# The widths of the last chunk's blocks and the step of the later chunks' exponentials, in an attention-and-two-MLPs kernel

## The chip, the cores and the metric

The kernel runs on one core of one Trainium2 chip. The metric is the device time of one execution in microseconds (us), as the median of several runs; the core's engines are TensorE (matrix products), VectorE, ScalarE, GpSimd and SyncE (it only issues DMAs). In the profile they are PE (matmuls) and PEld (the weight loads that go before them), DVE, ACT, POOL and SP.

## What is computed

12,480 tokens of width 128 pass through three stages. First an attention over 32 learned vectors ("inducing"), then an MLP with the activation h·cos(h), then an MLP with the activation h·sigmoid(h). Both MLPs go from 128 to 2048 and back to 128.

```python
def mab(q, kv):
    s = scale * (q @ kv.transpose(0, 2, 1))
    s = s - s.max(-1, keepdims=True)
    a = np.exp(s)
    a /= a.sum(-1, keepdims=True) + 1e-09
    return a @ kv
h = mab(I, x)                       # 32 x 128
x = mab(x, h)                       # 12480 x 128
h1 = x @ w_in1;  x = (h1 * np.cos(h1)) @ w_out1
h2 = x @ w_in2;  x = (h2 / (1 + np.exp(-h2))) @ w_out2
```

## The kernel before

A prologue of some 45 us loads x, transposes it and builds the 32 vectors h (the first `mab`). The rest, lines 724 to 1075, is a pipeline that this case is about.

**Tiling.** The 12,480 tokens are 98 tiles (97 whole ones and half a tile), and a tile is cut in four groups of 32 tokens. Tiles are gathered in seven chunks: 8 tiles, five times 16, and 10. A chunk is the unit of the second `mab`'s softmax. Its scores are 128 partitions (four groups of 32) by the chunk's columns, 512 for a chunk of 16 tiles.

A block is the unit of the MLPs: up to 512 token columns, given as pieces (group, first tile, tiles). The chunks of 16 tiles make four blocks of 512 columns each, one per group. The last chunk has 10 tiles with one group a little short, 1216 columns in all, and makes three blocks, numbers 22 to 24 of 25. Before the change these have 480, 448 and 288 columns (lines 263 to 267).

**Steps.** The 2048 hidden units are taken 256 at a time, so a block has eight units. The loop `for s in range(NU + L2 + D2 + 1)` does one step per unit; there are 200 units. In a full step TensorE runs 20 matmuls of the block's width, each with 128x128 fresh weights:

- `mlp1_in(s)`: 2 matmuls (line 763). ScalarE then makes the sine (798); VectorE multiplies (802), rounds to `hi` (809) and subtracts to `lo` (835).
- `mlp2_in(s - 11)`: 6 matmuls (line 898). ScalarE then makes the Silu (913) and `hi` (921), and GpSimd the `lo` (922).
- `mlp2_out(s - 13)`: 6 matmuls (`down`, line 845).
- `mlp1_out(s - 1)`: 6 matmuls (`down`, line 845).

All instructions stand in program order on their engine, by hand. The two accumulators of the down products have one PSUM buffer each, so the first matmul of a block's `mlp1_out` or `mlp2_out` waits until the block before has been read out of it.

**What comes at fixed steps of eight.** After `mlp2_out` of a block's last unit, at steps with s mod 8 = 4, `store` transposes the second accumulator on VectorE (945) and issues the output DMAs on SyncE (955, 961): four for each piece of the block, and one more where a piece holds the half tile. After `mlp1_out` of a block's last unit, at s mod 8 = 0, `y_split` copies the first accumulator: `yhi` on ScalarE (879), `ylo` on VectorE (880); from step 11 on it stands behind the step's `lo` (835) on VectorE. `fill` lets SyncE copy the softmax into a block's stacked operand, four DMAs a piece (298).

**The softmax of chunks 2 to 6** is spread over twelve steps that begin 24 steps before the chunk's first unit. For chunk 2 (whose first unit is step 48; 32 steps later for each of the next four) the table `later` puts "take" at step 24, "centre" at 26, "exp" at 28, "norm" at 30, "turn" at 34, "split" at 35. "exp" is one ScalarE instruction (243), issued right after the step's sine. "norm" is three VectorE instructions (247 to 249), issued at the end of its step, and a GpSimd multiply (250).

`held_back` moves `mlp2_in` of nearby steps to a later place among the matmuls: in the step after "exp" it goes to place 2, behind `mlp2_out` and `mlp1_out`; in the second step after it, and in the step after "take", to place 1, behind `mlp2_out`.

Of the kernel before, what the change touches and what calls it, by code (L numbers as in the profile page):

```python
# [22 lines left out]
def tile_induced_attention_then_two_mlps(  # L23
# [45 lines left out]
    FIRST, LAST, MT = 8, 10, 4  # L69
# [190 lines left out]
    blocks, first_of = [], []  # L260
    for k, (t0, nt) in enumerate(chunks):
        first_of.append(len(blocks))
        if k == NK - 1:
            half = nt // 2
            blocks += [(k, [(0, t0, nt), (3, t0, half)])]
            blocks += [(k, [(1, t0, nt), (3, t0 + half, nt - half)])]
            blocks += [(k, [(2, t0, nt)])]
        elif k > 0:
            blocks += [(k, [(g, t0, nt)]) for g in range(G)]
        else:  # L270
            for t in range(t0, t0 + nt, MT):
                m = min(MT, t0 + nt - t)
                blocks.append((k, [(g, t, m) for g in range(G)]))
# [30 lines left out]
    with ExitStack() as pro:  # L304
# [266 lines left out]
        for i in range(1, end):  # L571

            k = i - 2
# [164 lines left out]


    second = {3: "take", 5: "centre", 12: "exp", 12.25: "norm", 13: "turn", 14: "split"}  # L740
    later = {0: "take", 2: "centre", 4: "exp", 6: "norm", 10: "turn", 11: "split"}

    def d1(u):
        return 2 if u < WHOLE1 else 1
# [365 lines left out]
```

## Time and profile before

| | us |
|---|---|
| median of 3 runs (lowest, highest) | 958.15 (957.73, 958.24) |
| the profiled execution's own time | 957.71 |
| its span, first to last instruction | 955.5 |
| PE busy | 941.5 (99%) |
| DVE busy | 778.2 (81%) |
| ACT busy | 691.9 (72%) |
| POOL busy | 516.1 (54%) |

The granted TensorE clock has a mean of 0.999 of full speed. The engines run beside each other, so their busy times don't add up to the span. PE's matmuls overlap: one is listed with a duration longer than the distance to the next one, so what a matmul costs is read from the distance of starts and not from the durations.

### The profile page before, as it was taken

The numbers are of one execution on the slowest core, as the hardware profiler recorded it, in microseconds if no ns is written. First come the engines' busy times: TensorE is split into PE (matmuls) and PEld (weight loads), VectorE is DVE, ScalarE is ACT, GpSimd is POOL, SyncE is SP. The second block draws the span as 40 slices with busy tenths as digits, with TensorE's granted clock in tenths as the row PEclk, the third lists the DMA queues.
The fourth block names the chain that finished last, engine by engine and source line by source line (L and its number), as shares of the span: only waits on it lengthen the run. The fifth ranks groups of instructions, "written<-read, shape, count | busy, mean of one in ns | idle before, by whom it ended". The sixth has DMA issues, their size and how long they took to land.

```text
span 955.5 us, 11951 instructions
## 1 busy us (share of the span) xinstructions
PE 941.5 (99%) x4480; PEld 757.7 (79%) x4481; DVE 778.2 (81%) x784; ACT 691.9 (72%) x725; POOL 516.1 (54%) x274
## 2 busy tenths in 40 slices
PE   8899999999999999999999999999999999999997
PEld 5456778888878888878888887888887888888896
DVE  4889888988887988887988887988888888878751
ACT  5688668777768777767777777777767777777774
POOL 3346545655545655554655554665554655555565
PEclk9999999999999999999999999999999999999999
DMA  9341000010010010010010010010010100100001
GB/s 346 127 139 45 4 20 11 9 25 18 5 22 12 12 23 12 12 22 12 12 23 12 12 22 12 12 23 9 14 22 1 23 17 6 21 14 4 12 11 21
DMA packets 65484, 28.19 MB, mean 30 GB/s; under 512 B 54440, under 2 KB 60040, under 8 KB 65416
## 3 DMA queue, kind: packets, MB, share of 16 engines
q1 hardware_dynamic: 64760, 27.24, 10.9%
q8 instruction: 37, 0.61, 0.3%
q14 instruction: 31, 0.25, 0.1%
q10 hardware_dynamic: 656, 0.09, 0.1%
HBM read 14.79 MB, written 6.39 MB: 22 GB/s over the span
## 4 chain that ended last, share of the span: by engine, by line
PE 96%; DMA 2%; DVE 1%; issue 0%; ACT 0%; SPq 0%; POOL 0%; ACTq 0%; POOLq 0%; DVEq 0%
PE acc L845 53%; PE h L898 28%; PE h L763 9%; PE acc L855 4%; DMA x_sb<-in_x_dram 2%; PE s L213 1%; PE pt L394 0%; PE hp L541 0%; PE s L421 0%; DVE et L509 0%; SPq L330 0%; DVE c L802 0%; DVE mx L434 0%; PE misc L457 0%; POOL lo L927 0%
## 5 line engine op out<-in xcount | busy, mean ns | idle before, releaser
L922 POOL TENSOR_TENSOR lo<-s,hi 128x1024 fp32r<-128x1024 f32 (+3 forms) x189 | 445.6, 2358 | 372.7 <-ACT hi L921 351.9
L845 PE MATMUL acc<-hi,wo 128*128 128x512 f32 (+3 forms) x1520 | 401.7, 386 | 0.0
L845 PEld LDWEIGHTS acc<-hi,wo 128*128 128x128 f32 x1520 | 282.6, 188 | 59.8 <-issue 3.9
L798 ACT ACTIVATE c<-h,half_pi 128x1024 f32<-128x1024 f32 (+3 forms) x200 | 219.2, 1096 | 141.4 <-PE h L763 141.4
L802 DVE TENSOR_TENSOR h<-h,c 128x1024 f32<-128x1024 f32 (+3 forms) x188 | 226.1, 1203 | 115.3 <-ACT c L798 115.0
L913 ACT ACTIVATE s<-h 128x1024 f32<-128x1024 f32 (+3 forms) x200 | 201.1, 1006 | 73.7 <-PE h L898 69.9
L898 PE MATMUL h<-yhi,wi 128*128 128x512 f32 (+3 forms) x800 | 242.5, 385 | 0.0
L845 PE MATMUL acc<-lo,wo 128*128 128x512 f32 (+3 forms) x760 | 230.2, 384 | 0.1
L809 DVE CAST hi<-h 128x1024 fp32r<-128x1024 f32 (+3 forms) x188 | 224.8, 1196 | 6.5
L835 DVE TENSOR_TENSOR lo<-h,hi 128x1024 fp32r<-128x1024 f32 (+3 forms) x188 | 223.9, 1191 | 5.7
L921 ACT CAST hi<-s 128x1024 fp32r<-128x1024 f32 (+3 forms) x189 | 195.9, 1036 | 6.0
L898 PEld LDWEIGHTS h<-yhi,wi 128*128 128x128 f32 x800 | 148.9, 188 | 28.7 <-issue 0.5
L845 PEld LDWEIGHTS acc<-lo,wo 128*128 128x128 f32 x760 | 141.8, 188 | 27.9 <-POOL lo L927 0.4
L898 PE MATMUL h<-ylo,wi 128*128 128x512 f32 (+3 forms) x400 | 153.6, 384 | 0.0
L763 PE MATMUL h<-stk,hw 128*128 128x512 f32 (+3 forms) x400 | 125.8, 396 | 1.4 <-ACT stk L706 0.7
L763 PEld LDWEIGHTS h<-stk,hw 128*128 128x128 f32 x400 | 74.1, 188 | 24.9 <-issue 6.7
L898 PEld LDWEIGHTS h<-ylo,wi 128*128 128x128 f32 x400 | 75.1, 188 | 14.5
L945 DVE STREAM_TRANSPOSE o<-acc 128x512 f32<-128x512 f32 (+3 forms) x25 | 17.3, 693 | 9.4 <-PE acc L845 9.4
L879 ACT CAST yhi<-acc 128x512 fp32r<-128x512 f32 (+3 forms) x25 | 14.4, 577 | 14.0 <-PE acc L845 14.0
L855 PE MATMUL acc<-c,wf 128*128 128x512 f32 x48 | 22.5, 592 | 0.0
L880 DVE TENSOR_TENSOR ylo<-acc,yhi 128x512 fp32r<-128x512 f32 (+3 forms) x25 | 16.7, 668 | 5.4 <-ACT yhi L879 5.3
L802 DVE TENSOR_TENSOR c<-h,c 128x1024 f32<-128x1024 f32 x12 | 14.6, 1215 | 2.4 <-ACT c L798 1.9
(133 smaller groups left out, 318.7 us busy)
## 6 DMA issues: line engine op xcount, KB each, us to landing
out_dram<-o SPq DMA_DIRECT2D x80, 64.0 KB, 1.9
x_sb<-in_x_dram SPq DMA_DIRECT2D x8, 512.0 KB, 9.6
raw<-in_moe_w_in_dram SPq DMA_DIRECT2D x8, 512.0 KB, 7.3
raw<-in_moe_w_out_dram SPq DMA_DIRECT2D x8, 512.0 KB, 4.2
stk<-ahi SPq DMA_DIRECT2D x40, 64.0 KB, 2.0
stk<-at SPq DMA_DIRECT2D x40, 64.0 KB, 2.0
x_sb<-in_x_dram SPq DMA_DIRECT2D x3, 256.0 KB, 3.9
x_sb<-in_x_dram SPq DMA_DIRECT2D x2, 320.0 KB
```

Of the source, the lines that this page charges most:

```text
L763: nc.tensor.matmul(ps[:, a, 0:n], lhsT=hw[f // 4][:, f % 4 * P : (f % 4 + 1) * P], rhs=stacks[b][:, 0:n], start=True, stop=True,)
L798: nc.scalar.activation(cs, h, AF.Sin, bias=half_pi, scale=1.0)
L802: nc.vector.tensor_tensor(cs if whole else h, h, cs, ALU.mult)
L809: nc.vector.tensor_copy(hi[:, :, 0:n], h)
L835: nc.vector.tensor_tensor(lo[:, :, 0:n], h, hi[:, :, 0:n].bitcast(F32), ALU.subtract)
L845: nc.tensor.matmul(acc[:, 0:n], lhsT=wt[:, 2 * j + a, :], rhs=gt[:, a, 0:n], start=(j == 0 and p == 0 and a == 0), stop=(j == NJ - 1 and p ...
L855: nc.tensor.matmul(acc[:, 0:n], lhsT=w[:, 2 * j + a, :], rhs=c[:, a, 0:n], start=(j == 0 and a == 0), stop=(j == NJ - 1 and a == 1),)
L898: nc.tensor.matmul(ps[:, a, 0:n], lhsT=wt[:, fs], rhs=yt[:, 0:n], start=(p == 0), stop=(p == 2),)
L913: nc.scalar.activation(sv, hid2.pop(u)[:, :, 0:n], AF.Silu)
L921: nc.scalar.copy(hv, sv)
L922: nc.gpsimd.tensor_tensor(lv, sv, hv.bitcast(F32), ALU.subtract)
L945: nc.vector.transpose(o.rearrange("p t d -> p (t d)")[:, 0:n], acc2.pop(b)[:, 0:n])
```

## The change

The last chunk's three blocks get 512, 512 and 192 columns. The second block now has three pieces: all of group 1, the last four tiles of group 3 and the first three of group 2; the third block has the other seven tiles of group 2. Block 23 so gets twelve operand DMAs in place of eight and thirteen output DMAs in place of nine. And "exp" and "norm" of chunks 2 to 6 come a step later (29 and 31 for chunk 2); `held_back` is computed from "exp", so its places move with it, to steps 30 and 31.

```diff
         if k == NK - 1:
-            half = nt // 2
-            blocks += [(k, [(0, t0, nt), (3, t0, half)])]
-            blocks += [(k, [(1, t0, nt), (3, t0 + half, nt - half)])]
-            blocks += [(k, [(2, t0, nt)])]
+            cut = nt - MT
+            blocks += [(k, [(0, t0, nt), (3, t0, cut)])]
+            blocks += [(k, [(1, t0, nt), (3, t0 + cut, MT), (2, t0, MT - 1)])]
+            blocks += [(k, [(2, t0 + MT - 1, nt - MT + 1)])]
...
-    later = {0: "take", 2: "centre", 4: "exp", 6: "norm", 10: "turn", 11: "split"}
+    later = {0: "take", 2: "centre", 5: "exp", 7: "norm", 10: "turn", 11: "split"}
```

## Rows read from the trace of the kernel before

**Rows 1.** The page, part 1: busy us, share and instructions of each engine.

```profile
PE 941.5 (99%) x4480; PEld 757.7 (79%) x4481; DVE 778.2 (81%) x784; ACT 691.9 (72%) x725; POOL 516.1 (54%) x274
```

**Rows 2.** The page, part 4: the chain that ended last, by engine.

```profile
PE 96%; DMA 2%; DVE 1%; issue 0%; ACT 0%; SPq 0%; POOL 0%; ACTq 0%; POOLq 0%; DVEq 0%
```

**Rows 3.** Timeline of PE, steps 28 to 30: start us, us, engine, line, operation.

```profile
149.34 0.62 PE L763 MATMUL h<-stk,hw 128*128 128x512 f32 x2
...
153.88 0.61 PE L763 MATMUL h<-stk,hw 128*128 128x512 f32 x2
154.41 1.17 PE L845 MATMUL acc<-hi,wo 128*128 128x512 f32 x4
...
158.61 0.61 PE L763 MATMUL h<-stk,hw 128*128 128x512 f32 x2
```

**Rows 4.** Timeline of DVE, steps 28 to 33.

```profile
153.56 0.70 DVE L945 STREAM_TRANSPOSE o<-acc 128x512 f32<-128x512 f32 x1
...
165.69 0.68 DVE L247 TENSOR_REDUCE sm<-s 128x16 f32<-128x512 f32 x1
...
166.94 1.21 DVE L802 TENSOR_TENSOR h<-h,c 128x1024 f32<-128x1024 f32 x1
...
170.58 1.22 DVE L802 TENSOR_TENSOR h<-h,c 128x1024 f32<-128x1024 f32 x1
...
174.24 0.68 DVE L880 TENSOR_TENSOR ylo<-acc,yhi 128x512 fp32r<-128x512 f32 x1
```

**Rows 5.** Timeline of PE, step 33: its first matmul and its `mlp1_out`.

```profile
172.21 0.61 PE L763 MATMUL h<-stk,hw 128*128 128x512 f32 x2
...
175.38 1.07 PE L845 MATMUL acc<-hi,wo 128*128 128x512 f32 x4
```

**Rows 6.** Timeline of PE, step 192: twelve matmuls of 480 columns, six of 448.

```profile
896.18 0.60 PE L898 MATMUL h<-yhi,wi 128*128 128x480 f32 x2
...
898.79 0.98 PE L845 MATMUL acc<-hi,wo 128*128 128x448 f32 x4
...
900.01 0.30 PE L763 MATMUL h<-stk,hw 128*128 128x288 f32 x1
```

**Rows 7.** Timeline of PE, steps 205 and 207, block 24 alone.

```profile
937.85 0.29 PE L898 MATMUL h<-ylo,wi 128*128 128x288 f32 x1
938.19 0.77 PE L845 MATMUL acc<-hi,wo 128*128 128x288 f32 x4
...
940.63 0.43 PE L898 MATMUL h<-yhi,wi 128*128 128x288 f32 x2
...
942.21 0.29 PE L898 MATMUL h<-yhi,wi 128*128 128x288 f32 x1
```

**Rows 8.** Timeline of PEld and PE, prologue: matmuls of 128 columns with fresh weights.

```profile
43.51 0.52 PEld L699 LDWEIGHTS st<-lo,pick 128*128 128x128 f32 x4
...
43.55 0.62 PE L699 MATMUL st<-lo,pick 128*128 128x128 f32 x4
```

**Rows 9.** Timeline of all engines, the last matmul and what follows it.

```profile
947.66 0.97 POOL L927 TENSOR_TENSOR lo<-s,hi 128x288 fp32r<-128x288 f32 x1 [0.46 <-POOL lo L927]
948.68 0.19 PEld L845 LDWEIGHTS acc<-lo,wo 128*128 128x128 f32 x1 [0.36 <-POOL lo L927]
948.69 0.40 PE L845 MATMUL acc<-lo,wo 128*128 128x288 f32 x1
949.12 0.48 DVE L945 STREAM_TRANSPOSE o<-acc 128x288 f32<-128x288 f32 x1 [1.16 <-PE acc L845]
```

**Rows 10.** Timeline of PE: the last matmul of the last `mlp2_in`.

```profile
946.03 0.30 PE L898 MATMUL h<-ylo,wi 128*128 128x288 f32 x1
```

**Rows 11.** Timeline of DVE: block 23's store, step 204.

```profile
937.39 0.65 DVE L945 STREAM_TRANSPOSE o<-acc 128x448 f32<-128x448 f32 x1 [8.00 <-PE acc L845]
```

**Rows 12.** Timeline of SyncE's queue (SPq): block 23's output DMAs.

```profile
938.07 2.56 SPq L955 DMA_DIRECT2D out_dram<-o  x4
...
941.29 1.90 SPq L955 DMA_DIRECT2D out_dram<-o  x4
```

## The prediction

> **What bounds the kernel now.** I read the page's part 1 first: PE is busy in 99% of the span, no other engine in more than 81% [rows 1]. Then the chain that ended last: 96% of it is PE [rows 2]. So outside the prologue the time is TensorE's, in two kinds: matmuls, each worth the distance from its start to the next start, and the few waits in between. I looked for these by the starts of line 763's first matmul in each step, since a full step has 20 matmuls of 512 columns. Step 28 lasts 153.88 - 149.34 = 4.54 us, or 0.227 a matmul, and nearly all full steps are like it. Step 29 lasts 158.61 - 153.88 = 4.73 [rows 3]. Such a step follows each of the five "exp" steps of chunks 2 to 6 (0.17 to 0.20 us too long each), and besides the steps of the scores, which have more matmuls, no other step of the middle is long.
>
> **The exponentials: what goes.** In step 29 `mlp2_in` is held back, so `mlp2_out` of a new block stands right behind the two matmuls of `mlp1_in`. It would be due at 153.88 + 2 x 0.227 = 154.33. It starts at 154.41 and its first matmuls are slow [rows 3], because it needs the second accumulator, and the transpose of step 28's store runs to 153.56 + 0.70 = 154.26 on VectorE [rows 4]. From the transpose's end to where PE is back on its beat, 154.33 + 0.20 = 154.53, is 0.27. With "exp" at step 29 the held-back steps are 30 and 31, and in step 29 six matmuls (1.36 us) stand between again. The wait goes: 5 x 0.19 = -0.95 us. Nothing is late behind it at steps 30 and 31, as their Silu, `hi` and `lo` come in the same order, one step later.
>
> **The exponentials: what comes.** "norm" moves too, from step 30 to 31, and its VectorE part stands at the end of its step. In before it begins at 165.69, and the next step's multiply at 166.94, so it holds VectorE for 1.25 us [rows 4]. VectorE is already late then, since step 29's sine came late, behind "exp" and a Silu. It works without a gap from there: multiply of step 31 at 166.94, of step 32 at 170.58 (3.64 a step against 4.53, so it wins back 0.9 us a step), `ylo` of step 32 from 174.24 to 174.92 [rows 4]. `ylo` frees the first accumulator, and `mlp1_out` of the next block is due at 175.38, which is 3.17 into step 33 [rows 5]. Here the wait is hidden, by 0.46 us less the 0.27 above.
>
> After the change one step to catch up is missing between "norm" and `ylo`. Count from the start E of the step with "exp" (149.34 in before). "norm" starts 165.69 - 158.61 = 7.08 into its step [rows 3, 4], now the third from E: E + 9.07 + 7.08 = E + 16.15. The next step's multiply comes 1.25 later, at E + 17.40; and from that multiply to the end of `ylo` it is 174.92 - 170.58 = 4.34, so E + 21.74. `mlp1_out` is due at four steps and 3.17: E + 18.13 + 3.17 = E + 21.30. It gets back on its beat at 21.74 + 0.27 = E + 22.01, 0.7 us late. What is queued behind it on PE is the next step's `mlp1_in`, so the whole pipeline is late by it. At 0.69 a chunk: 5 x 0.69 = +3.45 us. Bounds: 0 (VectorE catches up in a way I don't see) and 5 x 1.0 (the wait in full with 0.3 more of lateness).
>
> **The widths.** Each block has 8 units of 20 matmuls, 160. At 480 columns a matmul costs (898.79 - 896.18) / 12 = 0.2175, at 448 (900.01 - 898.79) / 6 = 0.2033 [rows 6], at 288 (942.21 - 940.63) / 12 = 0.1317 [rows 7], at 512 0.227 [rows 3]. Block 22 gains 160 x 0.0095 = +1.52 and block 23 160 x 0.0237 = +3.79, together +5.3 us. All of it is on the path, and the other engines have run full steps of 512 columns all along.
>
> Block 24 at 192 columns is not in the trace. By the line through 288 and 448 it would be 0.089; that is the lower end. But every matmul here has a fresh 128x128 weight load. In the prologue, where such matmuls have only 128 columns, the loads follow each other at (0.52 - 0.19) / 3 = 0.110 us and the matmuls no faster [rows 8, 9]. And at the very end, where a load and its matmul start together (948.68 and 948.69), the matmul lasts 0.40 and not 0.30 [rows 9, 10]: it waits some 0.10 for its weights. So a load takes about 0.11, 288 columns hide it and 192 don't. I take 0.110: 160 x (0.1317 - 0.110) = -3.47. The upper end: the 128 columns could be slow in themselves, at 0.110 / 128 a column, and 192 would take 0.165, dearer than 288. I hold to the load since the last matmul shows it without a narrow one. Net +1.84; ends -1.6 and +10.6.
>
> The Trainium skill ("TensorE: Matmul & The Clock Gate", section LDWEIGHTS) has a load take its columns over 1.2 GHz, an estimate of 0.107 for 128; the rows' 0.110 agree, and by it the net would be +1.4. The same page (section Back-to-back issue gap) gives 0.081 as the sustained spacing at 128 columns; by that the load would not bind at 192, which is the second rival below. The trace's 0.110 speaks against it.
>
> **The end.** From the last matmul of the last `mlp2_in` to the last matmul of all it is 948.69 - 946.03 = 2.66 us [rows 9, 10], by Silu, `hi` and GpSimd's `lo` (0.97), then matmul and transpose (0.48). If only `lo` and transpose shrink with the columns by a third, that is 0.48 less; if all does, 1.1. I take 0.7, of which 18 x 0.022 = 0.39 is already in the matmuls: -0.3. The handover of the second accumulator from block 23 to 24 is exposed now: due at 937.85 + 0.13, `mlp2_out` starts at 938.19, 0.15 after the transpose's end [rows 7, 11]. With the transpose at 0.70 and six covering matmuls at 0.110 in place of 0.132 it is 0.05 + 0.13 worse: +0.2 (0 to 0.3).
>
> **Cost nothing.** Block 23's four more operand DMAs go out behind its eight, on SyncE, which has five steps (over 20 us) for them. Its four more output DMAs cost 4 x 0.48 = 1.9 us of SyncE's queue: they now end at 943.2, some 6 us before the last transpose, which needs their buffer [rows 9, 12]. With block 24 shorter by some 2 us a part of that cover goes, not all; without it each further us would be on the end.
>
> **Sum** against the profiled execution's 957.71 (span 955.5, 2.21 around it): -0.95 + 3.45 + 1.84 - 0.3 + 0.2 = +4.24, so 961.95. The median of the runs stood 0.44 above the profiled one; I put half on top: 962.1.
>
> **Rivals.**
> (a) No new wait at `ylo`: the 0.19 go and nothing comes. 961.95 - 3.45 = 958.5. For it: in before the same handover had 0.19 us to spare [rows 4, 5]. Against it: VectorE's rows have no gap from 166.94 on, so lateness can't go away.
> (b) The weight load doesn't bind at 192 columns (0.089): 160 x 0.021 = 3.4 less, 958.5, not slower than before. It decides from 0.098 a matmul on: below that the time is within 0.2% of before. For it: 288 columns show no sign of a load. Against it: the 0.110 of [rows 8].
> (c) (a) and (b) together: 955.1, faster.
> (d) Narrow matmuls stream at half rate (0.165): 160 x 0.055 = +8.8, 970.8. For it: [rows 8] alone would allow it. Against it: the last matmul [rows 9].
>
> **How the numbers follow.** Forecast 0.64 (960.3 to 963.5), (a) 0.13, (b) 0.12, (c) 0.04, (d) 0.07. The likeliest gives 962.1. The range takes in (a) and (b) and leaves out (c) and (d): 958.0 to 964.5. Under 0.2% (1.9 us) can't be told from no change: slower means over 960.1, which is nearly all of the forecast (0.62) and (d): 0.69; (a) and (b) are no change: 0.25; faster 0.06.
>
> **What would show it.** Right: steps 29, 61, 93, 125, 157 at 4.53; steps 33, 65, 97, 129, 161 at about 5.2, with PE's wait put down to `ylo`; matmuls of block 24 spaced by 0.110; blocks 22 and 23 at 0.227. Wrong: steps 33 and their like at 4.53 (then (a)); a spacing of 0.09 (b) or 0.165 (d) in the last steps; a wait of the last transpose for DMAs.

## The result, and the profile after

The changed kernel takes 963.63 us (median of 4 runs, 962.73 to 964.08) against 957.94 for the kernel before in the same session: a ratio of 1.0057, 95% interval 1.0045 to 1.0070, so 4.3 to 6.7 us slower. The forecast was 962.1 us, slower. The profiled execution after took 962.73 us, with a span of 960.4 against 955.5.

Where the 4.9 us of span lie, by the starts of line 763's matmuls (steps 0 to 24 differ by 0.04):

| stretch | before | after | difference |
|---|---|---|---|
| start to step 0 | 44.90 | 44.64 | -0.26 |
| step 24 to 176 (the moved exponentials) | 695.79 | 697.84 | +2.05 |
| step 176 to the last matmul's start (the new widths) | 122.91 | 125.28 | +2.37 |
| last matmul's start to the end of the span | 6.81 | 7.61 | +0.80 |

The page's part 1 and part 4 after, the lines that answer to [rows 1, 2]:

```profile
PE 944.5 (98%) x4481; PEld 754.3 (79%) x4481; DVE 777.1 (81%) x784; ACT 691.4 (72%) x725; POOL 516.9 (54%) x274
...
PE 89%; DVE 6%; DMA 1%; ACT 1%; issue 1%; SPq 0%; ACTq 0%; DVEq 0%
```

PE's matmuls are the same in number but for one record, yet VectorE now has 6% of the chain, where PE alone had 96% before. A chain that leaves the bounding engine says that there is a wait in it, and the list of PE's waits names it (engine, line, who was waited for: us in total, times, longest):

```profile
PE acc L845 <- DVE ylo L880: 1.4, 5, 0.3
PE acc L845 <- DVE o L945: 0.3, 1, 0.3
```

There are five waits for `ylo`, one for each of chunks 2 to 6, and one for the transpose at the handover from block 23 to 24. Before, this list was empty from 70 us on, though step 29 lost 0.19 there: the list counts only idle time behind the end that the profile models for the matmul before, and in [rows 3] the late matmul starts at 154.41, ahead of that end, 153.88 + 0.61 = 154.49. Step 29 and step 33 on PE's timeline after, to hold against [rows 3, 5]:

```profile
153.58 0.62 PE L763 MATMUL h<-stk,hw 128*128 128x512 f32 x2
...
158.12 0.39 PE L763 MATMUL h<-stk,hw 128*128 128x512 f32 x1
...
171.72 0.62 PE L763 MATMUL h<-stk,hw 128*128 128x512 f32 x2
...
174.44 0.61 PE L845 MATMUL acc<-lo,wo 128*128 128x512 f32 x2
175.35 1.19 PE L845 MATMUL acc<-hi,wo 128*128 128x512 f32 x4 [0.30 <-DVE ylo L880]
176.39 0.63 PE L845 MATMUL acc<-lo,wo 128*128 128x512 f32 x2
176.85 0.39 PE L763 MATMUL h<-stk,hw 128*128 128x512 f32 x1
```

Step 29 is down to 4.54 us, step 33 is up from 4.53 to 176.85 - 171.72 = 5.13 (5.07 to 5.14 in the five). The 0.30 that the row names is only what exceeds the end of the matmul before, as the profile models it; the whole loss, 0.60, is read from the distance of the steps. VectorE's timeline shows why, against [rows 4]; GpSimd's instruction beside it is in the last line:

```profile
168.59 1.23 DVE L835 TENSOR_TENSOR lo<-h,hi 128x1024 fp32r<-128x1024 f32 x1
169.74 0.68 DVE L247 TENSOR_REDUCE sm<-s 128x16 f32<-128x512 f32 x1
170.44 0.32 DVE L248 TENSOR_SCALAR sm<-sm 128x16 f32<-128x16 f32 x1
170.80 0.25 DVE L249 RECIPROCAL sm<-sm 128x16 f32<-128x16 f32 x1
170.97 1.21 DVE L802 TENSOR_TENSOR h<-h,c 128x1024 f32<-128x1024 f32 x1
...
174.62 0.68 DVE L880 TENSOR_TENSOR ylo<-acc,yhi 128x512 fp32r<-128x512 f32 x1
...
168.32 2.42 POOL L922 TENSOR_TENSOR lo<-s,hi 128x1024 fp32r<-128x1024 f32 x1 [0.76 <-POOL lo L922]
```

"norm" at 169.74 is followed directly by the step whose end is `ylo`. `ylo` ends at 175.30, 21.72 after the start of the step with "exp" (153.58); PE's matmul, due at 171.72 + 3.17 = 174.89, starts at 175.35.

Block 24 after: step 200, where twelve wide matmuls stand between narrow ones, and steps 206 to 208, twelve matmuls of 192 columns each ([rows 6, 7] before):

```profile
929.20 0.59 PE L845 MATMUL acc<-hi,wo 128*128 128x192 f32 x4
...
929.85 0.66 PE L898 MATMUL h<-yhi,wi 128*128 128x512 f32 x2
930.34 0.39 PE L898 MATMUL h<-ylo,wi 128*128 128x512 f32 x1
...
932.65 0.59 PE L845 MATMUL acc<-hi,wo 128*128 128x192 f32 x4
...
944.77 0.39 PE L898 MATMUL h<-yhi,wi 128*128 128x192 f32 x2
...
946.12 0.39 PE L898 MATMUL h<-yhi,wi 128*128 128x192 f32 x2
...
948.79 0.39 PE L898 MATMUL h<-yhi,wi 128*128 128x192 f32 x2
```

Step 206 gives (946.12 - 944.77) / 12 = 0.1125 a matmul, the two steps behind it (948.79 - 946.12) / 24 = 0.111. The twelve wide ones between 929.85 and 932.65 take 2.80 us where 12 x 0.227 are 2.72: the first ones behind a narrow group are slow, the first two 930.34 - 929.85 = 0.49 and not 0.45.

### The profile page after: what moved, and what is told of

The parts are those of the page before. It is cut to its first block, busy times and chain, and to the rows that moved or that the text cites. A ratio compares the mean times of both kernels' runs of the same rounds, so it can differ in the third digit from the quotient of the medians.

```text
span 960.4 us, 11960 instructions
## 1 busy us (share of the span) xinstructions
PE 944.5 (98%) x4481; PEld 754.3 (79%) x4481; DVE 777.1 (81%) x784; ACT 691.4 (72%) x725; POOL 516.9 (54%) x274
## 4 chain that ended last, share of the span: by engine, by line
PE 89%; DVE 6%; DMA 1%; ACT 1%; issue 1%; SPq 0%; ACTq 0%; DVEq 0%
PE acc L845 49%; PE h L898 26%; PE h L763 9%; PE acc L855 4%; DMA x_sb<-in_x_dram 1%; DVE hi L809 1%; DVE lo L835 1%; DVE h L802 1%; ACT c L798 1%; PE s L213 1%; ACT s L913 1%; PE hp L541 0%; PE pt L394 0%; DVE sm L247 0%; DVE ylo L880 0%
## 5 line engine op out<-in xcount | busy, mean ns | idle before, releaser
L922 POOL TENSOR_TENSOR lo<-s,hi 128x1024 fp32r<-128x1024 f32 (+1 forms) x189 | 447.3, 2367 | 376.0 <-ACT hi L921 348.8
L845 PE MATMUL acc<-hi,wo 128*128 128x512 f32 (+1 forms) x1520 | 402.6, 387 | 1.7 <-DVE ylo L880 1.4
L798 ACT ACTIVATE c<-h,half_pi 128x1024 f32<-128x1024 f32 (+1 forms) x200 | 219.3, 1097 | 144.8 <-PE h L763 144.4
L802 DVE TENSOR_TENSOR h<-h,c 128x1024 f32<-128x1024 f32 (+1 forms) x188 | 226.1, 1203 | 118.0 <-ACT c L798 117.7
L913 ACT ACTIVATE s<-h 128x1024 f32<-128x1024 f32 (+1 forms) x200 | 201.1, 1006 | 75.1 <-PE h L898 72.3
L898 PE MATMUL h<-yhi,wi 128*128 128x512 f32 (+1 forms) x800 | 243.1, 386 | 0.0
L845 PE MATMUL acc<-lo,wo 128*128 128x512 f32 (+1 forms) x760 | 230.6, 384 | 0.0
L809 DVE CAST hi<-h 128x1024 fp32r<-128x1024 f32 (+1 forms) x188 | 224.8, 1196 | 6.5
L835 DVE TENSOR_TENSOR lo<-h,hi 128x1024 fp32r<-128x1024 f32 (+1 forms) x188 | 223.9, 1191 | 5.7
L921 ACT CAST hi<-s 128x1024 fp32r<-128x1024 f32 (+1 forms) x189 | 195.6, 1035 | 6.1
```

The costliest lines, as they stand in the source:

```text
L798: nc.scalar.activation(cs, h, AF.Sin, bias=half_pi, scale=1.0)
L802: nc.vector.tensor_tensor(cs if whole else h, h, cs, ALU.mult)
L809: nc.vector.tensor_copy(hi[:, :, 0:n], h)
L835: nc.vector.tensor_tensor(lo[:, :, 0:n], h, hi[:, :, 0:n].bitcast(F32), ALU.subtract)
L845: nc.tensor.matmul(acc[:, 0:n], lhsT=wt[:, 2 * j + a, :], rhs=gt[:, a, 0:n], start=(j == 0 and p == 0 and a == 0), stop=(j == NJ - 1 and p ...
L898: nc.tensor.matmul(ps[:, a, 0:n], lhsT=wt[:, fs], rhs=yt[:, 0:n], start=(p == 0), stop=(p == 2),)
```

## The experiments

The kernels ran in two sessions, the first four in one and the last four in the other, with 25 and 33 runs of the kernel before (957.83 and 957.71 us). A difference in us is that of the medians.

**The widths alone.** This is the change without its second hunk.

```diff
-    later = {0: "take", 2: "centre", 5: "exp", 7: "norm", 10: "turn", 11: "split"}
+    later = {0: "take", 2: "centre", 4: "exp", 6: "norm", 10: "turn", 11: "split"}
```

> Widths 512, 512, 192; the exponentials stay at their old step. The two halves of the change add up, is the theory: steps 33, 65, 97, 129, 161 at 4.53 us and steps 29 to 157 at 4.7 as before; steps 176 to 191 at 4.53 each, 2.4 us more than before in all; block 24's matmuls 0.112 apart; the stretch from the last matmul to the end of the span 0.8 us longer than before, as in the changed kernel. In all +3.2 us (+2.5 to +4). Rival: the extra time at the end is chance, then +2.4 and an end as long as before.

It took 960.30 us, ratio 1.0023 (1.0013 to 1.0033), +2.5. That is nearer to the rival's +2.4 than to the theory's +3.2, and the end takes 7.03 us in its profile: not 0.8 but 0.2 longer than before. Steps 176 to 191 last 4.53 us, and from step 176 to the last matmul it is 125.28, to the hundredth what the changed kernel has. The wait is back in its old place:

```profile
153.76 0.61 PE L763 MATMUL h<-stk,hw 128*128 128x512 f32 x2
154.29 1.16 PE L845 MATMUL acc<-hi,wo 128*128 128x512 f32 x4
...
158.49 0.62 PE L763 MATMUL h<-stk,hw 128*128 128x512 f32 x2
```

**The exponentials alone.** This is the change without its first hunk.

> Only the move of the exponentials and norms by a step; widths 480, 448, 288. Theory: five times 0.41 to 0.45 us: the wait at steps 29 to 157 goes (4.53), steps 33 to 161 last 5.1, the end of the span is as before. In all +2.1 us (+1.6 to +2.6). Rival: the move is worth nothing by itself, 0.

It took 960.37 us, ratio 1.0023 (1.0014 to 1.0032), +2.5. From step 24 to 176 it is 697.92, 2.13 more than before; the waits are those of the changed kernel:

```profile
PE acc L845 <- DVE ylo L880: 1.5, 5, 0.3
```

So each half costs over 2 us by itself, and 1.0023 x 1.0023 = 1.0046 lies within the change's interval.

**"norm" behind `ylo`.** The exponentials come a step later than before, "norm" two; the widths are the old ones.

```diff
-    later = {0: "take", 2: "centre", 4: "exp", 6: "norm", 10: "turn", 11: "split"}
+    later = {0: "take", 2: "centre", 5: "exp", 8: "norm", 10: "turn", 11: "split"}
```

> Exponentials a step later as in the change, but norm two steps later (step 32 for chunk 2), so that its three VectorE instructions stand behind ylo; old widths. Theory (it is norm's 1.25 us on VectorE ahead of ylo that makes mlp1_out wait): steps 29 and 33 and their like all at 4.53, ylo ends about E + 20.5 and not 21.7 (E: start of the step with the exponential), -0.9 us in all (-0.6 to -1.2). Rival (the exponential's own lateness on ScalarE reaches ylo, wherever norm stands): steps 33 to 161 still at 5.1, +2.1 us.

It took 956.87 us, ratio 0.9988 (0.9979 to 0.9997), -1.0, as the theory had it. Steps 29 and 33 and their like all last 4.53 us, and PE's list of waits is empty. On VectorE "norm" now stands behind `ylo`; the step began at 171.97 on PE and `ylo` ends at 174.33, before the 175.15 at which PE wants the accumulator and gets it:

```profile
173.65 0.68 DVE L880 TENSOR_TENSOR ylo<-acc,yhi 128x512 fp32r<-128x512 f32 x1
174.24 0.68 DVE L247 TENSOR_REDUCE sm<-s 128x16 f32<-128x512 f32 x1
174.96 0.17 DVE L248 TENSOR_SCALAR sm<-sm 128x16 f32<-128x16 f32 x1
...
175.15 1.07 PE L845 MATMUL acc<-hi,wo 128*128 128x512 f32 x4
```

**"norm" one step behind "exp".** "norm" keeps its old step 30, with "exp" at 29; the widths are the old ones.

```diff
-    later = {0: "take", 2: "centre", 4: "exp", 6: "norm", 10: "turn", 11: "split"}
+    later = {0: "take", 2: "centre", 5: "exp", 6: "norm", 10: "turn", 11: "split"}
```

> Exponentials a step later, norm at its old step 30 (one step behind the exponential); old widths. Theory: VectorE has one step more to catch up between norm and ylo, ylo ends near E + 21.1, 0.6 us earlier than with the change; steps 33 to 161 at 4.55 to 4.65, steps 29 to 157 at 4.53; in all -0.3 to -0.8 us. Rival (the exponential's lateness alone): steps 33 to 161 at 5.1, +2.1 us.

It took 962.22 us, ratio 1.0046 (1.0032 to 1.0059), +4.4: a miss, and worse than the rival. Step 32 lasts 4.96 us and step 33 5.17. VectorE's and GpSimd's timelines, and in the first the matmul at which step 32 loses its time:

```profile
165.52 0.67 DVE L247 TENSOR_REDUCE sm<-s 128x16 f32<-128x512 f32 x1
166.23 1.43 DVE L248 TENSOR_SCALAR sm<-sm 128x16 f32<-128x16 f32 x1
167.69 0.25 DVE L249 RECIPROCAL sm<-sm 128x16 f32<-128x16 f32 x1
167.86 1.21 DVE L802 TENSOR_TENSOR h<-h,c 128x1024 f32<-128x1024 f32 x1
...
170.36 1.22 DVE L835 TENSOR_TENSOR lo<-h,hi 128x1024 fp32r<-128x1024 f32 x1
...
171.64 0.74 PE L845 MATMUL acc<-lo,wo 128*128 128x512 f32 x2
```

```profile
165.22 2.40 POOL L922 TENSOR_TENSOR lo<-s,hi 128x1024 fp32r<-128x1024 f32 x1 [1.88 <-issue]
168.03 1.05 POOL L250 TENSOR_TENSOR s<-s,sm 128x512 f32<-128x512 f32 x1 [0.40 <-DVE sm L249]
```

The add of 1e-9 to 16 elements a partition takes 1.43 us, and ends at 167.66, 0.04 after GpSimd's `lo` (165.22 + 2.40 = 167.62). Behind `ylo`, where GpSimd is idle, it takes 0.17; in the changed kernel 0.32, again ending 0.03 after GpSimd's instruction. So "norm" cost 2.3 us of VectorE here and not the 1.25 that I had taken as fixed, and the lateness that it brings was 1.1 us larger than expected. So late, VectorE makes PE wait twice: in step 33 for `ylo`, as in the changed kernel, and in step 32 already for the `lo` of step 31, which ends at 170.36 + 1.22 = 171.58, just before the matmul that reads it starts (171.64).

**The same without the add.** This kernel leaves out the 1e-9 of the second attention's sums.

```diff
     nc.vector.tensor_reduce(out=sm, in_=e, axis=AX.X, op=ALU.add)
-    nc.vector.tensor_scalar_add(sm, sm, 1e-9)
     nc.vector.reciprocal(sm, sm)
```

> As the run with norm at its old step 30, but norm's second VectorE instruction (the 1e-9 added to the second attention's sums) is left out, so the output differs by that. Theory (this instruction waits until GpSimd's running lo is through, 1.43 us in place of 0.18; the reduce and the reciprocal don't wait so): norm takes about 1 us of VectorE, the next multiply starts at E + 12.9, ylo ends near E + 20.9; steps 29, 32, 33 and their like all within 0.1 of 4.53; -0.9 us in all. Rival (any small VectorE instruction waits there): the reciprocal takes the 1.4 us, steps 32 and 33 stay at 4.96 and 5.17, +4.4 us.

It took 956.66 us, ratio 0.9989 (0.9980 to 0.9998), -1.0, with no waits on PE. The line numbers are one lower here. Reciprocal (0.25) and the next multiply run on while GpSimd's `lo` does (165.76 to 168.16), so it is the add alone that waits:

```profile
166.04 0.68 DVE L247 TENSOR_REDUCE sm<-s 128x16 f32<-128x512 f32 x1
166.75 0.25 DVE L248 RECIPROCAL sm<-sm 128x16 f32<-128x16 f32 x1
166.92 1.20 DVE L801 TENSOR_TENSOR h<-h,c 128x1024 f32<-128x1024 f32 x1
```

```profile
165.76 2.40 POOL L921 TENSOR_TENSOR lo<-s,hi 128x1024 fp32r<-128x1024 f32 x1 [1.92 <-issue]
```

The Trainium skill ("SBUF — State Buffer", section Who interferes with whom) says that a `tensor_scalar` can take a second port that VectorE shares with GpSimd and then waits for the whole of a GpSimd instruction that was issued first, while a `tensor_reduce` never does. The rows of the two runs agree: 1.43 us for the add and 0.67 for the reduce, both beside GpSimd's `lo`.

**Other widths**, all with "norm" behind `ylo`. The first is 512, 416 and 288, with as many pieces as before:

```diff
-            half = nt // 2
-            blocks += [(k, [(0, t0, nt), (3, t0, half)])]
-            blocks += [(k, [(1, t0, nt), (3, t0 + half, nt - half)])]
+            cut = nt - MT
+            blocks += [(k, [(0, t0, nt), (3, t0, cut)])]
+            blocks += [(k, [(1, t0, nt), (3, t0 + cut, MT)])]
             blocks += [(k, [(2, t0, nt)])]
```

> Norm behind ylo, and the last chunk's blocks at 512, 416 and 288 columns with as many pieces as before. Theory: -0.95 us from the steps, and 160 matmuls each of +0.0095 (480 to 512) and -0.0145 (448 to 416 by the line through 288 and 448): -0.8, -1.75 us in all (-1.2 to -2.3). Rival (only the sum of the columns counts): -0.95.

It took 956.03 us, ratio 0.9981 (0.9972 to 0.9990), -1.7: some 0.2% below the kernel before, and the lowest of all. From step 176 to the last matmul it is 121.83 us, 1.08 less than before. That the widths have a part in the gain, besides "norm", is shown by this stretch, not by the medians, whose intervals overlap with those of the two runs above that took 1.0 off.

Then comes the change's own form, with one and with two tiles of group 2 in the second block in place of three: 512, 448, 256 and 512, 480, 224. The edit for the first, against the changed kernel:

```diff
-            blocks += [(k, [(1, t0, nt), (3, t0 + cut, MT), (2, t0, MT - 1)])]
-            blocks += [(k, [(2, t0 + MT - 1, nt - MT + 1)])]
+            blocks += [(k, [(1, t0, nt), (3, t0 + cut, MT), (2, t0, 1)])]
+            blocks += [(k, [(2, t0 + 1, nt - 1)])]
```

> Norm behind ylo, blocks of 512, 448 and 256 columns. Theory (a weight load of 0.112 binds only below some 244 columns): 256 columns cost 0.117 a matmul, so +1.5 - 2.35 = -0.85 for the widths and -1.8 us in all (-1.2 to -2.4). Rival (narrow matmuls are slow in themselves, from 256 columns down): 0.15 or more, +3 us or more.

It took 956.81 us, ratio 0.9992 (0.9983 to 1.0001): -0.9, half of what was expected and outside the range given. The rival's 0.15 a matmul is out. A matmul of 256 columns costs (942.51 - 941.07) / 12 = 0.120 and not 0.117, and the stretch from step 176 to the last matmul, 122.69, is 0.22 less than before and not 0.85.

```profile
941.07 0.40 PE L898 MATMUL h<-yhi,wi 128*128 128x256 f32 x2
...
942.51 0.40 PE L898 MATMUL h<-yhi,wi 128*128 128x256 f32 x2
```

> Norm behind ylo, blocks of 512, 480 and 224 columns. Theory (the load binds): block 24's matmuls 0.112 apart as at 192 columns; widths +1.5 + 2.3 - 3.15 = +0.6, in all -0.3 us (-0.8 to +0.3). Rival (no load bound, the line goes on): 0.103 apart, -0.9 for the widths and -1.8 in all.

It took 957.44 us, ratio 0.9997 (0.9988 to 1.0006), -0.3, as the theory had it. At 224 columns a matmul costs (942.38 - 941.04) / 12 = 0.112, as at 192 and, but for 0.002, at 128 in the prologue [rows 8]; so somewhere between 256 and 224 columns a narrower block stops saving anything. The stretch is 123.58, 0.67 more than before.

```profile
941.04 0.38 PE L898 MATMUL h<-yhi,wi 128*128 128x224 f32 x2
...
942.38 0.38 PE L898 MATMUL h<-yhi,wi 128*128 128x224 f32 x2
```

## Why the prediction was right, step by step

- **The wait at steps 29 to 157 goes: right.** These steps all last 4.53 to 4.54 us.
- **A new wait for `ylo` at steps 33 to 161: right in place and cause, but taken a little too large.** `ylo`'s end was forecast at E + 21.74 and came at E + 21.72. The loss is 0.60 a chunk where 0.69 was taken (22.01 - 21.30 would be 0.71): I let PE need 0.27 us from the end of the VectorE instruction to be back on its beat, as it had behind the store's transpose; behind `ylo` it needs 0.19. With the old wait's 0.19 gone it makes 2.05 in place of 2.5 us. Rival (a) is out, and moving "norm" behind `ylo` shows the cause; so does leaving out the add.
- **"norm" holds VectorE for 1.25 us: right only at this distance.** It contains a wait for GpSimd, some 0.15 us here (the add takes 0.32, and 0.17 with GpSimd idle); at another step "norm" took 2.3. That the move left the 1.25 as it was is luck: nothing in the prediction asked what GpSimd does beside it.
- **Blocks 22 and 23 at 0.227 a matmul: right only while all blocks are wide.** Steps 176 to 191 last 4.53 us. From step 192 on they stand beside block 24, and the first ones behind a narrow group are slow. Added up from the starts in both traces, the matmuls of blocks 21 to 23 from step 176 on cost 5.84 us more than before, where 5.31 was forecast. The forecast was 0.53 too low, and had no term for this. The trace before had a sign: the steps behind the scores (25 and its like) last 140.28 - 135.60 = 4.68 us with 20 matmuls, though the prediction calls no such step long. Whether that is the same effect was not tested.

```profile
135.60 0.73 PE L763 MATMUL h<-stk,hw 128*128 128x512 f32 x2
...
140.28 0.62 PE L763 MATMUL h<-stk,hw 128*128 128x512 f32 x2
```

- **Block 24 at the weight load's pace, 0.110: right (0.111 to 0.1125).** Rivals (b), 0.089, and (d), 0.165, are out, and 224 columns cost the same as 192. That it is the load that sets the pace is argued, from the equal spacing at 128, 192 and 224 columns and the last matmul of [rows 9]; no run leaves the loads out. The Trainium skill ("TensorE: Matmul & The Clock Gate", section LDWEIGHTS) has a load take its columns over 1.2 GHz, an estimate of 0.107 for 128; the trace's 0.111 to 0.1125 nearly agree.
- **The end shorter by 0.3 and the handover longer by 0.2: both right.** From the last matmul of the last `mlp2_in` to the end of the last transpose it is 953.58 - 950.69 = 2.89 us, and before it was 949.60 - 946.03 = 3.57 [rows 9, 10]: 0.68 less, where 0.7 was taken, 0.39 of it counted with the matmuls. At the handover `mlp2_out` would be due at 943.52 + 0.11 and starts at 944.05, 0.42 late; before it was 0.21 [rows 7]. The last transpose is released by PE, and not by a DMA, so block 23's four more output DMAs cost nothing, as forecast.

```profile
943.52 0.28 PE L898 MATMUL h<-ylo,wi 128*128 128x192 f32 x1
944.05 0.33 PE L845 MATMUL acc<-hi,wo 128*128 128x192 f32 x1 [0.25 <-DVE o L945]
...
950.69 0.28 PE L898 MATMUL h<-ylo,wi 128*128 128x192 f32 x1
...
953.20 0.38 DVE L945 STREAM_TRANSPOSE o<-acc 128x192 f32<-128x192 f32 x1 [0.90 <-PE acc L845]
```

- **The 0.8 us behind the last matmul's start were not forecast, and the runs don't tie them to the change.** From the last transpose's end to the end of the span all kernels do the same. That takes 5.89 us before, 6.84 after, 6.25 with the same widths alone, and 6.63 with 512, 416 and 288 columns, whose last block is as wide as before. The last two DMA issues on SyncE take 1.44 us before, 2.07 after, and 1.85 with the exponentials alone, whose last block is the old one (in this order below). In all ten traces the second of them ends 0.4 to 0.6 us after a 16 KB transfer of the instruction queue q8 that runs beside it, and this transfer takes 0.93 us before and 1.40 after. It may set the length; no run varies it.

```profile
949.63 1.44 SPq L955 DMA_DIRECT2D out_dram<-o  x2
```

```profile
953.61 2.07 SPq L955 DMA_DIRECT2D out_dram<-o  x2
```

```profile
951.89 1.85 SPq L955 DMA_DIRECT2D out_dram<-o  x2
```

The measured median is 1.5 us over the forecast (961.95 and half of 0.44 would be 962.2, not 962.1). The interval (4.3 to 6.7 us) begins just above the forecast's +4.2, and the two halves run by themselves add up to +4.4 by their ratios and +5.0 by their medians. That the profiled execution, at 962.73, comes within 0.8 us of the sum's 961.95 is partly luck: the waits came 0.45 smaller than forecast, blocks 22 and 23 dearer by 0.53, what follows the last transpose by 0.95, and the prologue 0.26 shorter.

## What to carry to other kernels

When work in an in-order queue is moved away from one deadline, count the steps that remain between it and the next one: an engine that is late, and here wins back 0.9 us a step, pays for each step taken from it. Filling two blocks and leaving a narrow one pays only while the narrow one costs less for its fewer columns: with fresh weights for every matmul that ended here between 256 and 224. The cost of a small instruction read at one place of the schedule holds for that place: look at what runs on the other engines before taking it along.

## What was not expected of the hardware

- A VectorE `tensor_scalar` of 16 elements a partition took 0.17 us with GpSimd idle, and 0.3 to 1.8 us beside a GpSimd instruction, ending 0.03 to 0.04 us after it in all 25 cases (chunks 2 to 6 of five kernels). A reduce, a reciprocal and a `tensor_tensor` with one input in PSUM did not wait at the same place.
- With a fresh 128x128 weight load for each, matmuls of 128, 192 and 224 columns were all 0.11 us apart, those of 256 columns 0.120.
- The first matmuls of 512 columns behind a group of 192 were slow: 2.80 us for twelve in place of 2.72.
- The second of the last two DMA issues took 1.1 us before and 1.7 after, where issues ahead of it took some 0.45, and ended half a microsecond after a 16 KB instruction transfer beside it in all ten traces.
